# Attention weights of the second head mixing moved from GpSimd to VectorE, and a quarter of six tiles' score copies moved from VectorE to ScalarE

## The chip, the cores and the metric

One core of one Trainium2 chip. The metric is the device time of one execution in microseconds (us), lower is better. The engines are called as in the profile: PE (TensorE, with PEld for its weight loads), DVE (VectorE), ACT (ScalarE), POOL (GpSimd) and SP (SyncE, which here only issues transfers).

## The reference

Talking-heads attention over B = 2 batches, H = 12 heads, S = 448 positions, D = 64, and two feed-forward blocks behind it:

```python
scores = scale * np.matmul(q, k.transpose(0, 1, 3, 2))
scores = np.einsum('bhij,hg->bgij', scores, w_pre)        # first mixing of heads
scores = scores - np.max(scores, axis=-1, keepdims=True)
attn = np.exp(scores)
attn = attn / (np.sum(attn, axis=-1, keepdims=True) + 1e-09)
attn = np.einsum('bhij,hg->bgij', attn, w_post)           # second mixing of heads
out = np.matmul(attn, v)
# then x @ w_gate, silu, * (x @ w_val), @ w_out; then @ w_in, hard-swish, @ w_out
```

## The kernel before

**Two phases.** The attention runs over the first 206 us or so of the execution, the two feed-forward blocks (products of float32 split into a high and a low part) over the rest. Only the attention is touched by the change.

**Tiles and chunks.** The 448 query rows of each batch are cut into four tiles of 88 to 120 rows (`TILES`, t = 0 to 7 over both batches). `scores(t, c)` computes the scores of a pair of heads c (0 to 5) of tile t on PE into two PSUM banks, one for the even head (e = 0) and one for the odd (e = 1). `scores_out(t, c)` copies both banks into the tile's buffer `S0` or `S1` in SBUF (even tiles use `S0`, odd ones `S1`): the bank of e = 0 on DVE, that of e = 1 on ACT. The two banks carry the tag `pqk` with two buffers in all, so the next scores, or the next `av` (the product with v, same tag), wait for both copies.

**Relayout.** The mixing of heads wants heads on partitions. A chunk m is ten query rows; 90 chunks in all. `relayout(m)` moves eight of them from S to a buffer `sx` with a DMA issued on SP, `relayout_rest(m)` the last two with a DMA issued on POOL. Both need the whole tile copied out, the buffer of five pairs earlier free, and an earlier transfer landed that used the same semaphore. The rest of a tile is issued one step later than the tile's first part in program order (`i > scored[...]`).

**The step loop.** Step i (45 of them, two chunks each) issues in this order: `postmix(i)` (second mixing: 64 small matmuls on PE, 32 for each chunk, of the exponentials `e` with the chunk's weights `wn`); `exps` of the two chunks of step i + 1 (ACT); `attn_out(i)` (one copy on DVE, one on ACT); `weights` of the first chunk of step i + 1; the scores that are due in this step, with their copies; `weights` of the second chunk; `premix(i + 2)` (first mixing, PE, from `sx`) and two `row_max` (DVE); `av` where due; and at the step's end the copies `x_out` (DVE), the splits `x_split` (POOL, L324 and L326) and the relayouts. Each engine takes its instructions in that order. `weights(m)` is a chain: L242 adds 1e-9 to the sum, L243 takes the reciprocal (both DVE), and L245 multiplies the 128 x 60 table `W2` by it to give `wn`, on POOL. So POOL's queue holds L245, the splits and the DMA issues of `relayout_rest` in one line.

Scores of tiles 2 to 7 are spread over steps 2-7, 8-13, 13-17, 19-24, 24-29 and 30-35, `av` over 21 of the 45 steps, two pairs of heads each.

Of the kernel before, what the change touches and what calls it, by code (L numbers as in the profile page):

```python
# [12 lines left out]
ALU = mybir.AluOpType  # L13
# [34 lines left out]
def kernel(  # L48
# [14 lines left out]
    nc = tc.nc  # L63
# [66 lines left out]
    W2 = cst.tile([128, H, KG], F32, name="W2")  # L130
# [46 lines left out]
    def scores_out(t, c):  # L177
        n = TILES[t // 4][t % 4][2] * KI
        for e in range(2):
            h = 2 * c + e  # L180
            copy = nc.scalar.copy if e else nc.vector.tensor_copy
            copy(stiles[t][:n, h, :], pqk.pop((t, h))[:n, :S])  # L182

    sx = {}
# [54 lines left out]
    def weights(m):  # L239
        sm = ew[m][1]  # L240
        rc = pe.tile([128, 1], F32, name=f"rc{m}", tag="rc", bufs=6)
        nc.vector.tensor_scalar(rc, sm, 1e-9, None, ALU.add)  # L242
        nc.vector.reciprocal(rc, rc)  # L243
        wn = pe.tile([128, H, KG], F32, name=f"wn{m}", tag="wn", bufs=6)
        nc.gpsimd.tensor_scalar(wn, W2, rc, 1.0, ALU.mult, ALU.mult)  # L245
        wns[m] = wn

    def postmix(i):
# [227 lines left out]
    for t in range(2):  # L476
        for c in range(HP):
            scores(t, c, ("pqk", "ppre", "ppost", "ppre")[(6 * t + c) % 4])
            scores_out(t, c)
        if t == 0:  # L480
            load_q(0, 2, 3)
            for _ in range(8):
                relayout(placed)
                relayout_rest(placed)
                placed += 1
# [14 lines left out]
    def qk(t, c):  # L500
        scores(t, c)
        scores_out(t, c)
# [50 lines left out]
    for i in range(-LOOK, NP):  # L553
# [7 lines left out]
        for m in soft[:1]:  # L561
            weights(m)
        run(i, "qk")
        for m in soft[1:]:
            weights(m)
# [178 lines left out]
```

## Time and profile before

| What | us |
|---|---|
| median of three runs | 717.46 |
| lowest, highest | 711.99, 725.3 |
| the profiled execution's own time | 713.29 |
| its span, first to last instruction | 711.5 |
| PE busy in the span | 685.4 (96%) |
| DVE busy | 503.4 (71%) |
| ACT busy | 296.9 (42%) |
| POOL busy | 176.5 (25%) |

The profile is of one execution. Busy shares are means over two phases with different limits. A "wait" is idle time in front of an instruction, put down to what ended last before it. In the timelines the first column is the start in us from the span's start, the second how long the instruction, or the merged run of alike instructions (x8), took, and the bracket is the idle time before it with its releaser. PE's ends are modelled and overlap the next start, so PE's rows are read from start to start.

### The profile page before, as it was taken

The page shows a single profiled execution, that of the slowest core. Times are in us where ns is not written, and L with a number is a line of the kernel's source. Part 1 is how long each engine was busy: PE and PEld are TensorE (multiplying, and loading weights), DVE is VectorE, ACT ScalarE, POOL GpSimd, SP SyncE. Part 2 cuts the span into 40 slices and gives each one's busy share as a digit, 9 for nine tenths or more (in the row PEclk, how much of TensorE's full clock was granted, in tenths as well). Part 3 has the DMA queues.
Part 4 walks back from the last instruction along what each step waited for, and adds up shares of the span by engine and source line. Part 5 has one row for each costly group of instructions (what it writes and reads, how often), then busy time and mean ns, then how long its engine had stood idle before and what let it go on. Part 6 is the DMA issues. An engine that isn't in the chain of part 4 may idle for free.

```text
span 711.5 us, 16611 instructions
## 1 busy us (share of the span) xinstructions
PE 685.4 (96%) x6864; PEld 571.6 (80%) x6864; DVE 503.4 (71%) x853; ACT 296.9 (42%) x563; POOL 176.5 (25%) x275
## 2 busy tenths in 40 slices
PE   9699899799899999999999999999999999999997
PEld 3355565465579999999999999999999999999997
DVE  4676677688745888888888665668888888765550
ACT  4565466456543433434343322334445544333320
POOL 2444265454640221131112000002332332000000
PEclk9999999899999999999999999999999999999999
DMA  5777456443421424323242334232323323544420
GB/s 198 225 204 202 134 138 180 136 145 84 132 92 46 134 89 133 121 101 130 93 131 92 119 106 132 89 92 92 127 89 96 127 82 100 162 145 145 136 72 27
DMA packets 33629, 86.75 MB, mean 122 GB/s; under 512 B 9264, under 2 KB 21952, under 8 KB 33552
## 3 DMA queue, kind: packets, MB, share of 16 engines
q1 hardware_dynamic: 25632, 80.97, 35.3%
q0 software_dynamic: 7200, 3.94, 2.8%
q8 instruction: 54, 0.88, 0.5%
q10 hardware_dynamic: 720, 0.77, 0.3%
q14 instruction: 23, 0.19, 0.1%
HBM read 62.20 MB, written 2.75 MB: 91 GB/s over the span
## 4 chain that ended last, share of the span: by engine, by line
PE 87%; DMA 5%; issue 2%; DVE 2%; ACT 2%; POOL 1%; SPq 0%; POOLq 0%; ACTq 0%
PE pi L394 16%; PE pp L394 16%; PE po L394 12%; PE pg L394 12%; PE pv L394 12%; PE ppost L259 5%; PE pav L295 5%; PE pqk L166 4%; PE ppre L217 3%; DMA sx<-S 3%; DMA k<-in_k_dram 1%; PE p L394 1%; ACT e L236 1%; DMA q<-in_q_dram 1%; POOL wn L245 1%
## 5 line engine op out<-in xcount | busy, mean ns | idle before, releaser
L394 PE MATMUL pp<-g,hp 128*128 128x448 f32 x384 | 109.1, 365 | 0.0
L605 POOL TENSOR_TENSOR g<-rl,g 128x448 fp32r<-128x448 f32 x32 | 41.5, 1318 | 168.5 <-ACT g L604 168.5
L394 PE MATMUL po<-u,ho 128*128 128x448 f32 x288 | 81.7, 364 | 0.0
L236 ACT ACTIVATE e<-ppre,nm 128x448 f32<-128x448 f32 x90 | 56.4, 631 | 52.8 <-DVE nm L230 52.7
L259 PEld LDWEIGHTS ppost<-wn,e 60*64 60x64 f32 x2880 | 49.5, 137 | 34.3 <-POOL wn L245 29.7
L394 PEld LDWEIGHTS pp<-g,hp 128*128 128x128 f32 x384 | 72.0, 187 | 5.8
L605 POOL TENSOR_TENSOR u<-sg,u 128x448 fp32r<-128x448 f32 x24 | 32.9, 1391 | 151.2 <-ACT u L604 151.2
L394 PE MATMUL pi<-x2h,li 128*128 128x448 f32 x192 | 70.2, 366 | 0.0
L394 PE MATMUL pi<-x2l,hi 128*128 128x448 f32 x192 | 70.0, 364 | 0.0
L394 PE MATMUL pi<-x2h,hi 128*128 128x448 f32 x192 | 69.9, 364 | 0.0
L394 PE MATMUL pp<-g,lp 128*128 128x448 f32 x192 | 69.3, 361 | 0.0
L259 PE MATMUL ppost<-wn,e 60*64 60x60 f32 x2880 | 56.1, 224 | 12.5 <-POOL wn L245 11.3
L206 POOL DMA_DIRECT2D sx<-S x90 | 54.5, 606 | 33.9 <-issue 11.0
L230 DVE TENSOR_REDUCE nm<-ppre 128x1 f32<-128x448 f32 x90 | 51.7, 613 | 12.7 <-PE ppre L217 12.0
L394 PEld LDWEIGHTS po<-u,ho 128*128 128x128 f32 x288 | 54.1, 188 | 3.8
L217 PE MATMUL ppre<-sx,W 64*64 64x448 f32 x360 | 51.1, 558 | 4.6 <-DMA sx<-S 4.6
L166 PE MATMUL pqk<-k,q 64*64 64x448 f32 (+4 forms) x384 | 51.5, 570 | 2.6 <-ACT S L182 2.0
L394 PE MATMUL po<-u,lo 128*128 128x448 f32 x144 | 52.3, 363 | 0.0
L394 PE MATMUL pg<-xl,hg 128*128 128x448 f32 x138 | 50.5, 366 | 0.0
L394 PE MATMUL pv<-xl,hv 128*128 128x448 f32 x138 | 50.5, 366 | 0.0
L394 PE MATMUL pg<-xh,hg 128*128 128x448 f32 x138 | 50.5, 366 | 0.0
L295 PEld LDWEIGHTS pav<-at,v 128*64 128x64 f32 x768 | 36.9, 137 | 16.9 <-ACT S L182 11.8
(105 smaller groups left out, 1369.3 us busy)
## 6 DMA issues: line engine op xcount, KB each, us to landing
sx<-S SPq DMA_DIRECT2D x90, 182.0 KB
ri<-in_moe_w_in_dram SPq DMA_DIRECT2D x16, 768.0 KB
rg<-in_moe_w_gate_dram SPq DMA_DIRECT2D x12, 768.0 KB
rv<-in_moe_w_val_dram SPq DMA_DIRECT2D x12, 768.0 KB
ro<-in_moe_w_out_dram SPq DMA_DIRECT2D x12, 768.0 KB
rp<-in_moe_w_out_dram SPq DMA_DIRECT2D x12, 640.0 KB
rp<-in_moe_w_out_dram SPq DMA_DIRECT2D x6, 768.0 KB
sx<-S POOLq DMA_DIRECT2D x90, 42.0 KB, 4.9
```

The lines of the kernel that those rows point to most:

```text
L166: nc.tensor.matmul(p[e][lo:hi, :S], lhsT=qs[b][r, base + lo : base + hi], rhs=ks[b][r, c, :], start=True, stop=True, tile_position=(64 * e ...
L206: nc.gpsimd.dma_start(out=sx[m // 2][104:128, m % 2, :], in_=rows[8:, :H, :])
L217: nc.tensor.matmul(p[a][64 * r : 64 * r + 64, :S], lhsT=W1[rows, :], rhs=x[rows, r, :], start=True, stop=True, tile_position=(64 * a, 64 * r),
L230: nc.vector.tensor_reduce(nm, pre[m][:, :S], AX.X, ALU.max, negate=True)
L236: nc.scalar.activation(e[:, :S], pre.pop(m)[:, :S], AF.Exp, bias=tot.pop(m), scale=1.0, accum_out=sm)
L245: nc.gpsimd.tensor_scalar(wn, W2, rc, 1.0, ALU.mult, ALU.mult)
L259: nc.tensor.matmul(p[s][64 * c : 64 * c + 64, r, b, :, :], lhsT=e[rows, k0 : k0 + 64], rhs=wn[rows, :, :], start=True, stop=True, tile_pos ...
L295: nc.tensor.matmul(p[64 * e : 64 * e + 64, :n], lhsT=vs[b][:, jc, h, :], rhs=ats[t][:, jc, h, :n], start=jc == 0, stop=jc == JC - 1, tile_ ...
L394: nc.tensor.matmul(p[:, :S], lhsT=wt[:, kk, :], rhs=xx, start=start, stop=stop)
L605: eng.tensor_tensor(to[1], src, to[0].bitcast(F32), ALU.subtract)
```

## The change

Two edits. `weights` issues L245 on DVE, right behind the reciprocal, instead of on POOL. `scores_out` gives both copies to ACT for every odd pair of heads (c = 1, 3, 5) of tiles 2 to 7; that is 18 copies of e = 0 taken from DVE. Nothing else differs.

```diff
@@ scores_out
-            copy = nc.scalar.copy if e else nc.vector.tensor_copy
+            copy = nc.scalar.copy if e or (t > 1 and c % 2) else nc.vector.tensor_copy
             copy(stiles[t][:n, h, :], pqk.pop((t, h))[:n, :S])
@@ weights
         nc.vector.tensor_scalar(rc, sm, 1e-9, None, ALU.add)
         nc.vector.reciprocal(rc, rc)
         wn = pe.tile([128, H, KG], F32, name=f"wn{m}", tag="wn", bufs=6)
-        nc.gpsimd.tensor_scalar(wn, W2, rc, 1.0, ALU.mult, ALU.mult)
+        nc.vector.tensor_scalar(wn, W2, rc, None, ALU.mult)
         wns[m] = wn
```

On DVE, in step 15 (scores of tile 4, pair of heads 3; `rc32` and `wn32` belong to chunk 32):

```order
 L242 TENSOR_SCALAR rc32_1568<-sm32_1562 128x1
 L243 RECIPROCAL rc32_1568<-rc32_1568 128x1
-L182 COPY S0_107<-pqk4_3_0_1573 110x448
+L245 TENSOR_SCALAR wn32_1571<-W2_102,rc32_1568 128x60
 L242 TENSOR_SCALAR rc33_1581<-sm33_1564 128x1
 L243 RECIPROCAL rc33_1581<-rc33_1581 128x1
+L245 TENSOR_SCALAR wn33_1584<-W2_102,rc33_1581 128x60
 L230 TENSOR_REDUCE nm34_1592<-ppre17_0_1586 128x1
 L230 TENSOR_REDUCE nm35_1594<-ppre17_1_1587 128x1
```

The score copy has left DVE's line, and each reciprocal is followed by its own multiplication. In a step with an even pair the copy stays between the two groups and only the multiplications are added.

On POOL, from step 23 to step 26, where tile 5 (buffer `S1`) begins to be relaid (`sx28` holds chunks 56 and 57, its first two; `xh` and `xl` are the splits):

```order
-L245 TENSOR_SCALAR wn48_2241<-W2_102,rc48_2238 128x60
-L245 TENSOR_SCALAR wn49_2254<-W2_102,rc49_2251 128x60
 L324 TENSOR_TENSOR xl0_1520<-xs1_1334,xh0_1519 128x3x120
-L245 TENSOR_SCALAR wn50_2331<-W2_102,rc50_2328 128x60
-L245 TENSOR_SCALAR wn51_2352<-W2_102,rc51_2349 128x60
 L326 CAST xh0_1519<-xs2_1850 128x3x120
-L245 TENSOR_SCALAR wn52_2419<-W2_102,rc52_2416 128x60
-L245 TENSOR_SCALAR wn53_2432<-W2_102,rc53_2429 128x60
 L324 TENSOR_TENSOR xl0_1520<-xs2_1850,xh0_1519 128x3x120
 L206 DMA sx28_2367<-S1_108 24x1x448 x2
 L206 DMA sx29_2370<-S1_108 24x1x448 x2
```

What is left on POOL are splits and relayouts alone; the multiplications that stood in front of them, each behind a reciprocal of DVE, are gone.

## Rows read from the trace of the kernel before

**Rows 1.** The page, part 2: granted PE clock in 40 slices of 17.8 us.
```profile
PEclk9999999899999999999999999999999999999999
```

**Rows 2.** Stretch: busy us of PE, PEld, DVE, ACT, POOL; clock, DMA share, GB/s.
```profile
20.00:206.00 186.00, 165.60 (x4160) 101.36 (x4160) 132.90 (x398) 107.98 (x269) 95.05 (x198) 0.97 0.54 157
206.00:711.50 505.50, 501.11 (x2570) 463.48 (x2568) 362.08 (x441) 181.27 (x282) 75.12 (x57) 1.00 0.33 106
```

**Rows 3.** Timeline of step 15 into step 16: DVE, POOL and PE.
```profile
88.85 0.67 DVE L283 COPY at<-ppost 128x480 f32<-128x480 f32 x1 [0.81 <-PE ppost L259]
...
89.69 0.61 DVE L182 COPY S<-pqk 110x448 f32<-110x448 f32 x1
89.98 0.31 POOL L245 TENSOR_SCALAR wn<-W,rc 128x60 f32<-128x60 f32 x1 [0.30 <-DVE rc L243]
...
90.34 1.46 PE L259 MATMUL ppost<-wn,e 60*64 60x60 f32 x64
...
90.75 0.31 POOL L245 TENSOR_SCALAR wn<-W,rc 128x60 f32<-128x60 f32 x1 [0.46 <-DVE rc L243]
...
91.85 0.67 DVE L283 COPY at<-ppost 128x480 f32<-128x480 f32 x1 [0.25 <-PE ppost L259]
```

**Rows 4.** Timeline of PE: first mixings (ppre) of steps 26, 27, 32 and 33.
```profile
133.03 0.91 PE L217 MATMUL ppre<-sx,W 64*64 64x448 f32 x2
136.97 2.64 PE L217 MATMUL ppre<-sx,W 64*64 64x448 f32 x6 [3.03 <-DMA sx<-S]
...
142.35 1.29 PE L217 MATMUL ppre<-sx,W 64*64 64x448 f32 x8
...
161.51 1.47 PE L217 MATMUL ppre<-sx,W 64*64 64x448 f32 x6
163.93 0.96 PE L217 MATMUL ppre<-sx,W 64*64 64x448 f32 x2 [0.95 <-DMA sx<-S]
...
166.92 0.93 PE L217 MATMUL ppre<-sx,W 64*64 64x448 f32 x8
```

**Rows 5.** Timeline, 123 to 134 us: ACT's copy of tile 5's last pair, then POOL.
```profile
123.57 0.53 ACT L182 COPY S<-pqk 120x448 f32<-120x448 f32 x1
...
130.11 0.31 POOL L245 TENSOR_SCALAR wn<-W,rc 128x60 f32<-128x60 f32 x1 [0.47 <-DVE rc L243]
...
131.28 2.38 POOL L206 DMA_DIRECT2D sx<-S  x4
```

**Rows 6.** DMA issues, 0 to 210 us: KB each, median us from issue to landing.
```profile
sx<-S POOLq DMA_DIRECT2D x90, 42.0 KB, 4.9
```

**Rows 7.** Timelines of PE and POOL: waits at steps 3 and 38.
```profile
33.49 1.06 PE L259 MATMUL ppost<-wn,e 60*64 60x60 f32 x32 [2.79 <-POOL wn L245]
...
183.54 0.60 POOL L245 TENSOR_SCALAR wn<-W,rc 128x60 f32<-128x60 f32 x2
183.92 1.16 PE L259 MATMUL ppost<-wn,e 60*64 60x60 f32 x64 [1.53 <-POOL wn L245]
...
187.05 0.96 PE L217 MATMUL ppre<-sx,W 64*64 64x448 f32 x2 [0.62 <-DMA sx<-S]
```

**Rows 8.** Groups by line, 0 to 206 us: busy us, mean ns | idle before.
```profile
L182 DVE COPY S<-pqk 120x448 f32<-120x448 f32 (+3 forms) x48 | 29.5, 615 | 20.0 <-PE pqk L166 12.9 <-DMA sx<-S 4.0 <-PE ppre L217 1.9
...
L245 POOL TENSOR_SCALAR wn<-W,rc 128x60 f32<-128x60 f32 x90 | 27.7, 312 | 63.1 <-DVE rc L243 46.6 <-DVE rc L242 8.8 <-PE ppre L217 4.8
L182 ACT COPY S<-pqk 120x448 f32<-120x448 f32 (+3 forms) x48 | 25.6, 534 | 17.3 <-PE pqk L166 11.6 <-DMA sx<-S 4.2
...
L242 DVE TENSOR_SCALAR rc<-sm 128x1 f32<-128x1 f32 x90 | 12.7, 141 | 0.5 <-ACT e L236 0.5
```

**Rows 9.** DVE beside POOL in the second phase: timeline at 261 us.
```profile
261.16 0.55 DVE L368 TENSOR_SCALAR yg<-yg 128x768 f32<-128x768 f32 x1
261.39 2.79 POOL L605 TENSOR_TENSOR u<-sg,u 128x448 fp32r<-128x448 f32 x2 [10.91 <-ACT u L604]
261.75 1.41 DVE L369 TENSOR_SCALAR yg<-yg 128x768 uint32<-128x768 uint32 x1
```

## The prediction

> **What bounds the kernel now.** I read the busy times by stretch first. The last 505.5 us are TensorE alone: it is busy for 501.1 of them [rows 2], and no instruction of that phase changes. What the attention gains or loses should therefore reach the end one to one. In the 186 us from 20 to 206 no engine is full: PE 165.6, DVE 132.9, ACT 108.0, POOL 95.1 [rows 2]. So I went on to the timelines, and there two kinds of step differ.
>
> An ordinary step without a product with v is set by a round trip. In step 15 DVE copies `at` at 88.85, runs the first reciprocal, the score copy (89.69 to 90.30) and the second reciprocal; POOL multiplies the second weights at 90.75; the second mixing, a run of 1.16 where nothing holds it up [rows 7], is stretched to 1.46 by them; and the next `at` copy starts at 91.85, 3.00 later, after DVE had idled 0.25 for PE [rows 3]. PE's own work there is a run of 1.16 [rows 7], one of 0.93 for the first mixing [rows 4] and an equal one for the scores, 3.02 in all; the ends are modelled and each overlaps the next run's start by near 0.2, so 2.5 is my estimate.
>
> A few steps are far longer. The first mixing of step 26 starts at 133.03, and after two matmuls stops until 136.97 for a transfer into `sx`; the next step's starts at 142.35, 9.32 later instead of about 3 [rows 4]. Part of that is the clock: the slice from 124.5 to 142.3 is granted 8 tenths where its neighbours have 9 or more [rows 1], and the six matmuls after the wait take 2.64 where eight take 0.93 a little later [rows 4]. The transfer is late because of POOL. Tile 5 is copied out by 124.2 (the last copy starts at 123.57), but POOL issues its first two-row transfers only at 131.28, behind two multiplications that wait for DVE (the second at 130.11) and a split [rows 5]. The landing takes 4.9 [rows 6], and 131.28 plus 0.6 of issue plus 4.9 is 136.8, just when PE goes on.
>
> **The change part by part.**
>
> *The multiplication on DVE.* No row shows it there. From below: DVE's one-element operation takes 0.141 [rows 8] and its 768-element one 0.55 [rows 9], so 60 elements come to 0.141 + 59 x 0.41/767 = 0.173. From above: POOL's 0.312 [rows 8]. I take 0.18 and 0.02 of gap, 0.20, nearer the DVE rows. 90 of them are 18 us of DVE. Against it stands the hand-over: the reciprocal ends at about 89.77 and POOL's result at 90.29 [rows 3], so each weight comes about 0.3 earlier than now when DVE is next in line for it.
>
> *Score copies to ACT.* 18 copies of 0.615 leave DVE, 11.1 us; ACT gets 18 of 0.534, 9.6 us [rows 8]. DVE's balance is +6.9. ACT has about 78 us idle in the stretch [rows 2], which covers 9.6, except where the next scores wait for these very banks: twice (steps 13 and 24) an odd pair is followed by another pair in the same step. I charge 0.5 for the two together (from 0 to 2 x 0.53). Tile 5, for one, is complete 0.53 later for the same reason.
>
> *Ordinary steps.* By the loops of the code 24 of 45 steps have no product with v. In ten of them (3, 5, 7, 9, 15, 20, 22, 29, 31, 35) the pair of heads is odd: DVE's line is 2.75 busy now, less 0.53 (the copy, overlaps counted) plus 0.40 is 2.62, against PE's 2.50; the step falls from 3.00 to about 2.7, gain 10 x 0.3 = 3.0. In twelve others (0, 1, 2, 4, 10, 16, 26, 32, 37, 38, 41, 43) DVE only gets the 0.40: 2.75 + 0.40 = 3.15, loss about 0.2 each, 2.4. The 21 steps with a product with v have 32 more matmuls on PE, which hide it. Net gain 0.6; with each of these sizes off by half it lies between -3 and +4.
>
> *POOL set free.* This is where I see the gain. Without the multiplications POOL's queue no longer keeps pace with DVE: it issues a tile's rows as soon as the tile is copied out and the buffer is free.
> - Steps 26 to 27: issue moves from 131.28 to about 125, landing to about 131, before PE asks at 133. The excess is 9.32 - 3.0 = 6.3, the slow clock in it; I count 5.5, since PE may come for it up to 0.8 earlier. (Bounds: 0 if another transfer is last too, 6.3.)
> - Steps 32 to 33, tile 6: 161.51 to 166.92 is 5.41 [rows 4], excess 2.4; the same reason; I count 2.0 (0 to 2.4).
> - Step 38: the second mixing waits 1.53 for weights that stand behind POOL's transfers [rows 7]; I count 1.2. In the same step the first mixing waits 0.62 for `sx` [rows 7]; in step 32 a wait of 0.95 went with an excess of 2.4 [rows 4], so by that ratio 1.5; I count 1.3. (Together 0 to 3.0.)
> - Step 3: 2.79 lost, because the copies of tile 2 into `S0` wait until tile 0's last rows have left it [rows 7]. POOL can issue those about 2 us earlier, but SP moves the other eight rows of each chunk and I cannot see those land; I count 1.5 (0 to 3.5, with the clock behind it).
>
> Sum: 5.5 + 2.0 + 1.2 + 1.3 + 1.5 = 11.5 from POOL, 0.6 from the steps, less 0.5: 11.6. The profiled execution took 713.3, so 701.7. The median of the three runs, 717.46, stands 4.2 above that execution. Late landings are a likely part of what differs between runs, and the change takes away much of their effect, so I do not carry the 4.2 over and forecast 702.
>
> *A rule against it.* In the second phase DVE's L369 takes 1.41 while POOL's L605 runs, and the like operation just before it 0.55 [rows 9]. The Trainium skill, SBUF — State Buffer, section Who interferes with whom, says that VectorE in its two-port modes, which `tensor_scalar` from SBUF to SBUF can enter, and GpSimd share one port pair and that the later one blocks fully; by that rule, the trace agrees. The new multiplication is such an operation and could wait for a split or a transfer's issue on POOL. By that rule a few of the 90 would each lose some tenths; what that costs at most is worked out in the second rival.
>
> **The rivals.**
>
> *The waits for `sx` stay.* POOL's rows come earlier, but SP's eight rows of a chunk, or the DMA engines themselves (busy share 0.54 in the stretch [rows 2]), are as late. For it: SP waits for the same complete tile, which now comes 0.53 later. Against: issue time and landing of POOL's own rows explain 136.8 by themselves. Then only step 38's 1.2 and the steps' 0.6 less 0.5 are left: 713.3 - 1.3 = 712.
>
> *DVE becomes the bound.* If the score copies were never on the path and DVE's line were it in all steps, the balance of +6.9 would be paid: 720. If besides each multiplication that meets a long POOL operation waited like L369 (0.86 more than its neighbour [rows 9]), say one in ten of the 90, 9 x 0.86 = 7.7 more: 728. It decides from the point where DVE has no idle time in front of the `at` copy; now it has 0.25 in such a step [rows 3], and 53 us over the stretch [rows 2], which speaks against it. Place: the steps with even pairs and those after the scores are done.
>
> *More than counted.* Every excess vanishes (6.3 + 2.4 + 3.0 + 3.5 = 15.2) and the steps give 4: 713.3 - 19 = 694. For it: each of these waits has POOL's queue in front of it; against: shorter steps ask for the transfers sooner.
>
> **How the numbers follow.** Forecast (696 to 708) 0.65, waits stay 0.20, DVE the bound 0.08, more than counted 0.07. A difference of 2% is about what a measurement of this kernel can tell from no change. Measured from the median that line is at 703, from the profiled execution at 699, so it runs through the forecast: I give 0.35 of its 0.65 to faster and 0.30 to same. Faster 0.35 + 0.07 = 0.42; the first rival is all same, and of the second 0.03: same 0.30 + 0.20 + 0.03 = 0.53; slower 0.05. The range of 694 to 713 leaves out the second rival and the ends.
>
> **What would show it.** Right: POOL's transfers for tile 5 start within 2 us after ACT's last copy of that tile; PE's waits for `sx` (3.03, 0.95, 0.62) and the clock's dip at 124.5 to 142.3 are gone; the multiplication on DVE takes 0.17 to 0.20; odd steps come every 2.7, even ones every 3.2; the second phase still lasts 505. Wrong: first mixings still wait for transfers issued on SP; the multiplication takes over 0.3; DVE shows no idle time before the `at` copy even in steps with a product with v; or the copies of an odd pair on ACT hold back PE in more than the two steps named.

## The result, and the profile after

The changed kernel takes 710.3 us (median of 20 runs, 704.29 to 714.06); beside it the kernel before took 716.09 (20 runs, 711.99 to 725.3). The ratio is 0.9907, with a 95% interval of 0.9884 to 0.993: 6.7 us faster (0.0093 x 716.1). I had forecast 702. The profiled execution took 714.06, 3.8 above its median, which matters below.

The stretches that answer to [rows 2], and the clock row of the page that answers to [rows 1]:

```profile
20.00:206.00 186.00, 159.52 (x4137) 99.03 (x4138) 146.63 (x469) 114.20 (x286) 67.46 (x108) 0.98 0.53 158
206.00:711.50 505.50, 501.87 (x2602) 464.17 (x2598) 362.12 (x441) 181.18 (x282) 74.15 (x56) 1.00 0.33 106
...
PEclk9999999999999999999999999999999999999999
```

DVE's busy time rose by 13.7 us, ACT's by 6.2, POOL's fell by 27.6. The second phase lasts as before. The clock's dip in the slice from 124.5 us is gone.

What POOL was to give back, it gave. First POOL and ACT at the end of tile 5, then PE's first mixings of steps 26 and 27 (timelines of the kernel after; they answer to [rows 5] and [rows 4]):

```profile
128.82 0.97 ACT L182 COPY S<-pqk 120x448 f32<-120x448 f32 x2
...
130.19 1.24 POOL L206 DMA_DIRECT2D sx<-S  x2 [12.67 <-ACT S L182]
...
138.10 0.93 PE L217 MATMUL ppre<-sx,W 64*64 64x448 f32 x8
...
141.41 0.93 PE L217 MATMUL ppre<-sx,W 64*64 64x448 f32 x8
```

POOL has been idle for 12.67 us and issues 0.40 after ACT's last copy of the tile ended, where it was 7.2 late before. The two first mixings are 3.31 apart instead of 9.32, both in one piece.

But PE now waits for other things. PE's waits from 20 to 206 us, columns: line and releaser, us in total, times, longest; first of before, then of after:

```profile
PE ppost L259 <- POOL wn L245: 11.3, 13, 2.8
PE ppre L217 <- DMA sx<-S: 4.6, 3, 3.0
...
PE pav L295 <- ACT S L182: 0.8, 4, 0.2
PE pqk L166 <- issue: 0.4, 1, 0.4
```

```profile
PE pav L295 <- ACT S L182: 6.4, 9, 1.2
PE ppost L259 <- DVE rc L242: 5.5, 7, 1.2
PE ppost L259 <- issue: 4.7, 3, 2.1
PE ppost L259 <- DVE wn L245: 4.1, 3, 2.5
...
PE pqk L166 <- issue: 1.1, 1, 1.1
```

No wait for `sx` is left. The second mixing's waits for its weights, 11.3 us on POOL before, now end on DVE and are hardly shorter (5.5 + 4.1). Two waits are new: the product with v (`pav`) waits 6.4 us for ACT's score copies, where it was 0.8; and 5.8 us are put down to "issue", a stop that no semaphore explains, where it was 0.4.

An odd step without a product with v came out as worked out. Step 15 of after, DVE, to be held against [rows 3]:

```profile
92.22 0.68 DVE L283 COPY at<-ppost 128x480 f32<-128x480 f32 x1 [0.81 <-PE ppost L259]
...
93.18 0.25 DVE L245 TENSOR_SCALAR wn<-W,rc 128x60 f32<-128x60 f32 x1
...
93.73 0.25 DVE L245 TENSOR_SCALAR wn<-W,rc 128x60 f32<-128x60 f32 x1
...
94.96 0.66 DVE L283 COPY at<-ppost 128x480 f32<-128x480 f32 x1
```

It lasts 2.74 (94.96 - 92.22) instead of 3.00; I had said 2.7. DVE has no idle time in it any more: it sets this step. The even step 16 lasts 3.26, where I had said 3.2.

The groups by line over the whole span, to be held against [rows 8] (busy us, mean ns):

```profile
L182 ACT COPY S<-pqk 120x448 f32<-120x448 f32 (+3 forms) x66 | 33.4, 536 | 16.6 <-PE pqk L166 12.6 <-DMA sx<-S 1.8 <-PE ppre L217 1.4
...
L245 DVE TENSOR_SCALAR wn<-W,rc 128x60 f32<-128x60 f32 x90 | 27.6, 307 | 3.1
L182 DVE COPY S<-pqk 120x448 f32<-120x448 f32 (+3 forms) x30 | 18.6, 622 | 16.7 <-PE pqk L166 11.0 <-DMA sx<-S 4.1 <-PE ppre L217 0.3
```

A multiplication of the weights costs DVE 0.307 in the mean (the median is 0.253; seven of the 90 take 0.50 to 1.80), not 0.18 and a gap of 0.02.

**Where the time went, step by step.** DVE's 45 copies to `at` mark the steps. The table gives, for each class of step, how much the distances between these copies changed against the profile of before, in us; minus is a gain. Step 44 has no following copy and is left out. The first column is my sum sorted in the same way (step 3's 1.5 stands with the third class, since the wait lies between the copies of steps 2 and 3; the 0.2 a step of even steps is shared out).

```
steps                                       predicted  after     e1     e3     e6     e7
26, 32, 37, 38 (waits behind POOL)             -9.2    -8.45  -8.32  -8.68  -8.57  -7.68
3 5 7 9 15 20 22 29 31 35 (odd, no av)         -3.0    -1.70  +3.57  +1.37  -1.45  +2.69
0 1 2 4 10 16 41 43 (other, no av)             +0.1    +3.41  -0.48  -1.13  -0.13  +0.34
13, 24 (two pairs of scores)                   +0.5    -0.52  -0.55  -0.48  -0.02  -0.52
20 steps with a product with v                  0      +8.02  +1.25  -1.86  +0.83  +2.71
sum                                           -11.6    +0.76  -4.53 -10.78  -9.34  -2.46
```

In the profile of after the first class gave nearly what I had counted, and the last took it back. Each column is one execution with stops of its own, so its sum is not the difference of the medians: of the +3.41 of after, 1.78 is step 10, with a stop and a slow clock (last section), and 1.43 is step 43, with a multiplication held up beside POOL (e4). The columns e1, e3, e6 and e7 are experiments.

### The profile page after: what moved, and what is told of

Its sections match the earlier page's. It is cut to its first block, busy times and chain, and to the rows that moved or that the text cites. A ratio compares the mean times of both kernels' runs of the same rounds, so it can differ in the third digit from the quotient of the medians.

```text
span 712.3 us, 16449 instructions
## 1 busy us (share of the span) xinstructions
PE 679.8 (95%) x6864; PEld 570.3 (80%) x6864; DVE 517.3 (73%) x925; ACT 303.1 (43%) x581; POOL 147.9 (21%) x185
## 4 chain that ended last, share of the span: by engine, by line
PE 83%; DVE 8%; DMA 4%; ACT 2%; issue 2%; SPq 0%; POOL 0%; ACTq 0%; DVEq 0%; POOLq 0%
PE pi L394 16%; PE pp L394 16%; PE po L394 12%; PE pg L394 12%; PE pv L394 12%; PE pav L295 4%; PE pqk L166 4%; PE ppost L259 3%; DMA sx<-S 2%; DVE nm L230 2%; PE ppre L217 2%; DVE wn L245 2%; DMA q<-in_q_dram 2%; DVE at L283 1%; ACT e L236 1%
## 5 line engine op out<-in xcount | busy, mean ns | idle before, releaser
L206 POOL DMA_DIRECT2D sx<-S x90 | 52.1, 579 | 110.5 <-ACT S L182 37.2
L166 PE MATMUL pqk<-k,q 64*64 64x448 f32 (+4 forms) x384 | 53.3, 567 | 3.4 <-ACT S L182 1.9
L394 PE MATMUL pv<-xh,hv 128*128 128x448 f32 x138 | 50.4, 365 | 0.0
```

The lines of the kernel that those rows point to most:

```text
L166: nc.tensor.matmul(p[e][lo:hi, :S], lhsT=qs[b][r, base + lo : base + hi], rhs=ks[b][r, c, :], start=True, stop=True, tile_position=(64 * e ...
L206: nc.gpsimd.dma_start(out=sx[m // 2][104:128, m % 2, :], in_=rows[8:, :H, :])
L394: nc.tensor.matmul(p[:, :S], lhsT=wt[:, kk, :], rhs=xx, start=start, stop=stop)
```

## The experiments

Each ratio is against the kernel before on the same chip, with its 95% interval. The full change stands at 0.9907.

### One edit at a time: e1 and e2

```diff
 e1, against before
-        nc.gpsimd.tensor_scalar(wn, W2, rc, 1.0, ALU.mult, ALU.mult)
+        nc.vector.tensor_scalar(wn, W2, rc, None, ALU.mult)
 e2, against before
-            copy = nc.scalar.copy if e else nc.vector.tensor_copy
+            copy = nc.scalar.copy if e or (t > 1 and c % 2) else nc.vector.tensor_copy
```

> Only the weights' multiplication on DVE, score copies as before. Theory 1 (the gain comes from POOL's freed queue, and the ordinary steps get no shorter): PE's wait for sx at step 26, 3.03 before, is below 0.5, the step from first mixing to first mixing there 3.0 to 3.6, and the time is 0.985 to 1.00 of before: like the full change or a little slower, since DVE carries 18 copies more. Rival A (the copies on ACT are what made it faster): 1.00 or above, no better than before. Rival B (DVE's line is the bound): 1.01 or more.

> Only the 18 score copies on ACT, multiplication on POOL as before. Theory 1: PE still waits 2 to 4 us for sx at step 26 and 0.5 to 1.5 at steps 32 and 38; time 0.995 to 1.008 of before. Rival A: 0.985 to 0.995, as the full change.

Measured: e1 0.9971 (0.9949 to 0.9992), 2.1 us; e2 1.0009 (0.9988 to 1.003), nothing. PE's waits in e1, then in e2:

```profile
PE ppost L259 <- DVE wn L245: 5.8, 10, 2.6
PE pav L295 <- ACT S L182: 5.6, 8, 0.7
```

```profile
PE ppre L217 <- DMA sx<-S: 3.7, 4, 1.6
```

The weights on DVE alone take away every wait for `sx`, and the waits for DVE and for `pav` eat most of it. The copies alone leave PE waiting for `sx` (3.7 us, 4.6 before); that what the odd steps gain is waited for there fits this, but no run shows it. Together the edits gain 6.7, more than the 2.1 - 0.6 of the two apart: the copies pay clearly only beside the weights on DVE, which also make the transfers early.

### The transfers early, nothing moved: e3

```diff
-        while rests < placed and rests // 2 <= i + LOOK + 3 and i > scored[chunks[rests][0]]:
+        while rests < placed and rests // 2 <= i + LOOK + 3 and i >= scored[chunks[rests][0]]:
```

POOL issues a tile's two-row transfers one step earlier in its program; the multiplication stays on POOL.

> The kernel before with one comparison changed: the two-row transfers of a new tile are issued on POOL at the end of the step in which the tile is complete, not one step later, so two multiplications fewer stand in front of them; nothing moves between engines. Theory 1: the wait for sx at step 26 falls from 3.03 to under 1, those at steps 32 and 38 to under 0.5, and the time to 0.985 to 0.993 of before, as much as the full change gives, with no load on DVE. Rival A and a rival by which another transfer is last as well: 0.997 to 1.003, the waits stay.

Measured: 0.9875 (0.9841 to 0.9909), 8.9 us, by its middle more than the full change, within overlapping intervals. PE's waits from 20 to 206 us:

```profile
PE pav L295 <- ACT S L182: 1.2, 6, 0.2
...
PE ppre L217 <- DMA sx<-S: 0.5, 2, 0.3
```

The waits for `sx` are nearly gone and nothing took their place. So the early transfers alone give the whole gain, and POOL didn't have to lose the multiplication for it: it only had to take the transfers in another order.

### The full change without its lock: e4

DVE, not POOL, makes the low part of the first two blocks of weights (the subtraction of L385).

```diff
-        eng = nc.gpsimd if pool is pools["wp0"] else nc.vector
+        eng = nc.vector
```

> The changed kernel with the low part of the first two weight blocks subtracted on DVE instead of POOL (steps 42 and 43), so that no POOL operation of 1.8 us stands beside the last multiplications on DVE. Theory (the multiplication of 1.80 and PE's wait of 1.31 at step 44 are the shared port): no multiplication on DVE above 1.1, the wait of 1.31 gone, 0 to 2 us faster than the changed kernel, 0.987 to 0.992 of before. Rival (DVE's own later queue caused the wait): the wait stays within 0.3 of 1.31 and the time is as the changed kernel's or slower by about 1 us, the cost of two subtractions of 0.96 on DVE.

Behind it stood this place of the kernel after, at the end of the attention:

```profile
203.93 1.80 POOL L385 TENSOR_TENSOR lv<-yv,hv 128x768 fp32r<-128x768 f32 x1 [3.17 <-ACT hv L383]
203.98 1.80 DVE L245 TENSOR_SCALAR wn<-W,rc 128x60 f32<-128x60 f32 x1
...
205.84 0.69 PE L259 MATMUL ppost<-wn,e 60*64 60x60 f32 x32 [1.31 <-DVE wn L245]
```

A multiplication of 0.25 takes 1.80 beside a subtraction of POOL that began 0.05 earlier, and PE waits 1.31 for it. Measured in e4: 0.9898 (0.9863 to 0.9932); the multiplication there takes 0.25, and that wait of 1.31 is gone, so the lock is shown; another, of 1.35 at 102 us, stayed, where I had expected none above 1.1. The step from copy 43 to copy 44 is still 1.04 longer than before (1.43 in after), but in e4 most of it ran at the lower clock, granted 0.50 (columns as in [rows 2]):

```profile
197.20:200.40 3.20, 3.20 (x33) 2.37 (x30) 2.38 (x8) 1.33 (x2) 0.00 (x0) 0.50 0.02 5
```

So the step doesn't price the lock. The time can't be told from that of the full change: the middles differ by 0.6 us.

### Both together, and the copies with early transfers: e5 and e6

e5 is the full change with the edit of e3; e6 is e3 with the copies of e2, the weights on POOL.

> The full change, with the two-row transfers written one step earlier in POOL's program as well (the edit of e3). Theory (what the full change gains is the early transfers and nothing else, and it has them already): the ratio stays at that of the full change, 0.991 (0.988 to 0.994), and the wait of TensorE for ACT's score copies in steps with a product with v stays near 6 us. Rival (early transfers and relieved engines are two separate gains that add): 0.9907 x 0.9875, about 0.978.

> The kernel before with the earlier transfers of e3 and the score copies of odd pairs on ACT; the weights stay on POOL. Theory (with the transfers early the path runs over DVE and ACT in turn; copies alone moved nothing, 1.0009, since every gain ended in the waits for the transfers; now DVE's 11.1 us less and ACT's 9.6 us more about cancel): 0.984 to 0.991, the same as e3 within its interval. Rival 1 (the copies relieve DVE, as the way from e1, 0.9971, to the full change, 0.9907, suggests): 4.6 us better than e3, 0.981. Rival 2 (ACT's queue in steps with a product with v is the new bound): 0.993 or more.

Measured: e5 0.9878 (0.9848 to 0.9908), e6 0.9847 (0.9824 to 0.9869). The two gains don't add: e5 is not near 0.978. Its middle is 2 us below the full change, but the intervals overlap. The copies are worth 2.0 us on top of e3 (0.0028 x 714), again within overlapping intervals, and 4.6 on the way from e1 to the full change (0.0064 x 715), where they are clear. e5 against e6 also prices the weights on DVE as the change has them, with early transfers in both: 2.2 us (0.0031 x 714), within overlapping intervals.

### The price of DVE's time alone: e7

```diff
 e7, against e3
         nc.gpsimd.tensor_scalar(wn, W2, rc, 1.0, ALU.mult, ALU.mult)
+        spare = pe.tile([128, H, KG], F32, name=f"spare{m}", tag="spare", bufs=2)
+        nc.vector.tensor_scalar(spare, W2, rc, None, ALU.mult)
```

> The kernel of e3 plus a second, unused multiplication of the weights on DVE behind each reciprocal (90 of them); POOL still makes the weights that are used. It prices DVE's time alone, with hand-over and transfers as in e3. Theory (each pair of multiplications puts the row maxima of the step off by 0.4 to 0.6 us, and with them the exponentials, ACT's copies and the product with v): 5 to 9 us slower than e3, ratio 0.994 to 1.000, and waits of TensorE for ACT's score copies of 4 us or more. Rival (DVE has room, and what e1 lost against e3 is the lock with POOL or the transfers' order): within 2 us of e3, 0.985 to 0.990.

Measured: 0.9953 (0.9932 to 0.9974), 5.6 us slower than e3 (0.0078 x 714). The spare line of the groups, two `at` copies of step 15, and the new wait:

```profile
L247 DVE TENSOR_SCALAR spare<-W,rc 128x60 f32<-128x60 f32 x90 | 22.8, 253 | 3.1
```

```profile
89.62 0.67 DVE L285 COPY at<-ppost 128x480 f32<-128x480 f32 x1 [0.81 <-PE ppost L261]
...
92.92 0.67 DVE L285 COPY at<-ppost 128x480 f32<-128x480 f32 x1
```

```profile
PE pav L297 <- ACT S L182: 3.6, 8, 0.5
```

The step grew from 3.01 (e3) to 3.30, and `pav`'s wait for ACT from 1.2 (e3) to 3.6, a little less than I had expected. So 22.8 us more on DVE, used by nobody and hardly ever locked (none over 0.31), cost 5.6 us: 0.25 of a microsecond for each. This is the price of DVE's time where the weights are still handed over to POOL and DVE makes all copies of e = 0. The change spares the hand-over and the odd pairs' copies, and by e5 against e6 it pays less, 2.2.

### A shorter chain on DVE: e8, e9, e12

```diff
 in the three of them
-        nc.vector.tensor_scalar(rc, sm, 1e-9, None, ALU.add)
-        nc.vector.reciprocal(rc, rc)
+        nc.vector.reciprocal(rc, sm)
```

e8 is the full change with this, e9 is e6 with this, e12 is e5 with this. The addition of 1e-9 is left out in all three; the sum is at least 1 (the row's maximum gives exp(0)), so that in float32 it changes nothing.

> The full change with the addition of 1e-9 ahead of the reciprocal left out (90 DVE instructions of 0.14 us, a part of the computation that is not made); the rest is as in the full change. Theory (DVE's chain reciprocal, weights, row maxima is on the path in most steps): 90 x 0.14 to 0.17 is 13 to 15 us less on DVE, of which about a third to a half reaches the path: 4 to 7 us better than the full change, 0.981 to 0.985, and the waits for ACT's score copies fall from 6.4 to about 4. Rival (DVE is not on the path; ACT's and TensorE's own lines are): 0.989 to 0.993.

> The kernel of e6 (transfers early, score copies of odd pairs on ACT, weights on POOL) with the addition of 1e-9 left out as in e8. Theory (every microsecond taken from DVE ahead of the weights and the row maxima is worth 0.2 to 0.35 us; 13 to 15 us go): 3 to 5 us better than e6, ratio 0.977 to 0.981. Rival (with the weights on POOL, DVE has so much room that its time no longer counts): 0.983 to 0.987, as e6.

> The same with the weights on DVE, as in the change under study (e8 with the transfers one step earlier). Theory (DVE's 27 us of weights cost 0.2 to 0.3 each, less the hand-over to POOL that they spare): 2 to 5 us slower than e9, 0.982 to 0.987. Rival (with a shorter chain on DVE, sparing the hand-over weighs more than DVE's time): as fast as e9 or faster, 0.980 or less.

Measured: e8 0.9842 (0.9818 to 0.9865), e9 0.984 (0.9806 to 0.9875), e12 0.987 (0.984 to 0.99). With the weights on DVE, taking 12.7 us off its chain brings the full change 4.6 us (0.0065 x 715, clear of its interval), somewhat over the 3.2 that e7's price gives; e8's waits for `pav` fell only from 6.4 to 5.6, less than I had expected:

```profile
PE pav L294 <- ACT S L182: 5.6, 8, 0.7
```

With the weights on POOL the same edit brings nothing to be seen (e9 against e6: 0.5 us): the rival held there. And e12 against e5 shows 0.6 us within its interval, though it should have shown e8's 4.6. The three don't agree better than to some 4 us; that DVE's time is on the path rests on e7, and with the weights on DVE on e8, and e12 speaks for a smaller size. e12 against e9, the weights on DVE against those on POOL, is 2.1 us slower (0.003 x 715, within overlapping intervals), as e5 against e6. The fastest of all are e6, e8 and e9, 0.984 to 0.985, which can't be told apart.

### Step 3: e13

```diff
 e13, against e9: the scores of tile 2 at steps 3 to 8
-((2, 7), (8, 13), (13, 17), (19, 24), (24, 29), (30, 35))
+((3, 8), (8, 13), (13, 17), (19, 24), (24, 29), (30, 35))
```

> The kernel of e9 with the six scores of tile 2 at steps 3 to 8 instead of 2 to 7, which asks for S0 one step later. It looks at the wait of 2.5 to 2.8 us in step 3 that my forecast gave 1.5 us back. Theory (tile 0's last rows leave S0 near 32 us by the order of all transfers of the start, whoever issues them; a step later nobody waits for them): the wait of the second mixing at 33 us falls under 0.7, gain 1 to 2.5 us against e9. Rival (the start is bound by the transfers as a whole, so the wait turns up again a step later, or tile 2 now comes late): within 1 us of e9 or slower.

Measured: 0.9865 (0.9837 to 0.9892), no better than e9 and, by the middle, 1.8 us slower. The stretch from copy 2 to copy 3 is 3.41 us shorter than before (0.07 in e9), so the wait at step 3 went; but step 8, which now has two pairs of scores, grew by 2.56, and step 5 by 1.36. The rival held: the time turns up later.

### Stops of TensorE that nothing explains: e14

```diff
 e14, against after: in the first warm-up
+        for _ in range(20 if n == WARM[0] else 0):
+            nc.tensor.matmul(p[:, :16], lhsT=idle[:, :128], rhs=idle[:, :16], start=True, stop=True)
```

> The full change with 20 small extra matmuls (16 columns, and 20 weight loads with them) among TensorE's first warm-up matmuls, before any data has arrived: 40 more instructions on TensorE, nothing else. It looks at the idle times before TensorE's instructions that no semaphore explains: in the full change 2.12, 1.08, 0.54 and 2.05 us, and the same three or four matmuls resume so in e4 and e5 (the last 18, 2 and 53 matmuls of a second mixing, the last four of a pair of scores). Theory (TensorE's own program is fetched in packets of 16 KB, 256 instructions of 64 bytes, and TensorE stops at a packet's first instruction when the packet is late): the places move back by 20 matmuls with their weight loads, so that such idle times are found before the last 38 and the last 22 matmuls of a second mixing and no longer before the last 18, 2 or 53; each ends 1.3 to 1.7 us after a packet of the instruction queue has landed. Rival (they come from something that these instructions wait for and the profile does not show): the places stay, at the last 18, 2 and 53 matmuls. The time: as the full change, 0.988 to 0.994, unless the places now fall on less or more of the path, 2 us either way.

Measured: 0.9896 (0.9865 to 0.9927), as the full change. PE around two of these stops, first in after, then in e14:

```profile
191.88 1.15 PE L259 MATMUL ppost<-wn,e 60*64 60x60 f32 x60
193.57 0.27 PE L259 MATMUL ppost<-wn,e 60*64 60x60 f32 x2 [0.54 <-issue]
...
198.92 0.44 PE L259 MATMUL ppost<-wn,e 60*64 60x60 f32 x11
201.42 1.03 PE L259 MATMUL ppost<-wn,e 60*64 60x60 f32 x53 [2.05 <-issue]
```

```profile
188.53 0.81 PE L259 MATMUL ppost<-wn,e 60*64 60x60 f32 x40
190.44 0.57 PE L259 MATMUL ppost<-wn,e 60*64 60x60 f32 x24 [1.11 <-issue]
...
194.28 1.45 PE L295 MATMUL pav<-at,v 128*64 128x120 f32 x23
198.48 1.16 PE L295 MATMUL pav<-at,v 128*64 128x120 f32 x9 [2.76 <-issue]
```

The stop after 60 of the 64 matmuls of a second mixing (60 + 4) now comes after 40. The one after 11 now comes with 9 left of the 32 of the product before it: 11 + 9 is 20. Both moved back by exactly the 20 matmuls put in. The places belong to the program's order, not to the data. (I had named the places 18 and 2 as ones that should be empty; e14 has a stop before the last 18 and one before the last 2, but at other steps.)

## Why the prediction was wrong

The direction, the mechanism on POOL and the range of 694 to 713 held; the size did not, 6.7 us instead of 11.6, on a median that stood 2.8 above my base. Of the 8.3 us between 702 and 710.3, that base is 2.8; POOL's terms are 2.6 (11.5 counted, 8.9 in e3); the steps and copies are 2.3 (a gain of 0.6 - 0.5 counted, a loss of 8.9 - 6.7 = 2.2 measured). These are middles, each good to some 2 us; the rest is that the medians differ by 5.8 where the ratio says 6.7. That 710.3 lies beside the first rival's 712 is chance, since the waits for `sx` did not stay.

**Right: POOL's queue.** Transfers that start when the tile is complete, waits for `sx` and the dip of the clock gone, 8.45 of 9.2 us in the four steps. e3 shows that this alone gives the whole gain. Of the terms, step 26 gave 4.18 between its `at` copies (I counted 5.5, less 0.2), step 32 gave 2.15 (2.0), steps 37 and 38 gave 2.12 (2.5). **Step 3's 1.5 did not come**: PE still waits there, 2.48 where it was 2.79 [rows 7], because the copies into `S0` still wait for a transfer, and the stretch gained 0.53. Which transfer is last there was not tried. e13 shows that moving this wait away is no gain either.

```profile
31.93 0.62 DVE L182 COPY S<-pqk 120x448 f32<-120x448 f32 x1 [2.30 <-DMA sx<-S]
...
33.15 1.12 PE L259 MATMUL ppost<-wn,e 60*64 60x60 f32 x32 [2.48 <-DVE wn L245]
```

**Wrong: "The 21 steps with a product with v have 32 more matmuls on PE, which hide it."** This is the step that failed: it put the loss in these steps at nothing, and in after they lost 8.02 us. Of that 3.67 are stops and 1.24 a stretch at the lower clock (both below), and 1.11 is step 8, where the score copies waited for a transfer out of `S1`:

```profile
54.78 0.62 DVE L182 COPY S<-pqk 90x448 f32<-90x448 f32 x1 [1.77 <-DMA sx<-S]
```

The 2.0 that are left (about as much in e4's profile: 6.56 less 4.48 of stops) I put down to DVE and ACT. Step 30 of after shows the path:

```profile
152.12 1.15 DVE L230 TENSOR_REDUCE nm<-ppre 128x1 f32<-128x448 f32 x2
...
152.84 0.63 ACT L236 ACTIVATE e<-ppre,nm 128x448 f32<-128x448 f32 x1 [0.55 <-DVE nm L230]
...
153.46 0.62 ACT L236 ACTIVATE e<-ppre,nm 128x448 f32<-128x448 f32 x1
...
154.07 0.64 ACT L283 COPY at<-ppost 128x480 f32<-128x480 f32 x1
...
154.55 0.54 ACT L182 COPY S<-pqk 100x448 f32<-100x448 f32 x1
...
155.15 1.73 PE L295 MATMUL pav<-at,v 128*64 128x110 f32 x32 [0.67 <-ACT S L182]
```

The row maxima begin behind the weights on DVE; ACT's two exponentials wait for them; the copies of `at` and of the scores stand behind these in ACT's queue; and `pav` needs the bank that the score copy frees. PE has more matmuls in such a step, but it can't begin them. What the odd step ahead gained (2.74 for 2.98) was given back here (4.83 for 4.51). That DVE's time does this by itself is shown by e7, where these steps take 4.6 us more than in e3, 0.9 of them a stop; that it goes by way of ACT is read from the timelines and was not tried by itself, and e8, faster with hardly less of this wait, shows that the wait's sum is not its price.

**Mis-sized: the multiplication.** 0.20 with its gap, against 0.307 in the mean: 0.253 undisturbed, the rest beside POOL. The upper bound, POOL's 0.312, would have been the better choice, and at e7's price the 0.107 x 90 = 9.6 us are worth about 2.4, an estimate and rather an upper one. The odd steps, where I counted -3.0, gave -1.7. The rule of the Trainium skill on the shared port pair (SBUF — State Buffer, Who interferes with whom) did apply: 1.80 instead of 0.25 in the worst case, 27.6 - 90 x 0.253 = 4.8 us of DVE in all. Each of the seven long ones ends 0.05 to 0.06 us after an operation of POOL did. What they cost on the path is within the noise of e4 for the longest, and was not tried for the others.

**Right in part: the copies.** The 0.5 of steps 13 and 24 was not lost, and the relief of DVE in the odd steps is seen: -1.70 in after against +3.57 in e1, which lacks it. But e6 against e3, both with the weights on POOL, shows what the forecast left out: in their profiles the odd steps are 2.8 us shorter and the steps with a product with v 2.7 longer. `pav`'s wait for ACT rose there from 1.2 to 2.8:

```profile
PE pav L295 <- ACT S L182: 2.8, 7, 0.7
```

**Wrong: the base.** I did not carry over the 4.2 between the profiled execution and the median, as I took late landings for its cause. The waits for `sx` went and a spread of the same kind stayed (704.29 to 714.06), so they were not its main cause; over the kernels it goes with TensorE's stops (last section), which is no proof. The rival "DVE becomes the bound" was nearer than its 0.08: DVE does bind in the odd steps, yet 0.25 of each microsecond is paid in e7, not all.

By the ratios the parts meet in two ways. -8.9 (e3) + 5.6 (e7) - 2.0 to 4.6 (the copies) is -5.3 to -7.9, and 6.7 was measured. Or -8.9 - 2.0 (e6) + 2.2 (e5 against e6) is -8.7, which is e5, and the full change, whose transfers come one step later in POOL's program, is 2.0 short of it, within overlapping intervals. So DVE's price stays open between 2.2 and 5.6 us.

## What to carry to other kernels

When a transfer is late because its issue stands behind slow work in an engine's queue, try first to issue it earlier in that queue: here one character (e3) gave as much as moving 90 instructions to another engine, without the new owner's bill. An engine with idle time isn't free: follow what stands behind the added instruction through the next engines' queues up to the bottleneck, and price it with a spare copy of the instruction (e7) as well as with the swap itself (e5 against e6): here they gave 5.6 and 2.2 us. And where one profiled execution stands off the median, look for what differs before choosing the base.

## What the runs showed of the hardware

**TensorE stops for its own program.** The instruction queue moves packets of 16,384 bytes, 54 of them in each execution:

```profile
q8 instruction: 54, 0.88, 0.5%
```

54 x 16,384 bytes over 13,728 matmuls and weight loads (6864 of each on the page) are 64.4 bytes for one, so a packet holds some 256 instructions. In the profiles of the 14 kernels, before and after among them, TensorE stopped 40 times between 15 and 215 us for 0.3 us or more (up to 2.76) with "issue" as the releaser, and each time it went on 1.19 to 1.76 us after such a packet had landed, though only 33 or 34 of them come in these 200 us, one every 6 us. Counted over all of TensorE's instructions in the trace (matmuls, weight loads and the waits of its sequencer), all 40 stops stand at the same place of 256: 193 or 194 instructions behind a multiple of 256, in every one of the 14 kernels. The kernels after, e4 and e5, whose TensorE programs are alike, stop at the same matmuls (e5 at all four places of after, e4 at three), and e14 moves the matmuls there but not the count. So these stops are waits for the program itself. Most of the places are passed without one; why a packet comes late was not tried. The kernel before has 0.4 us of them, after 5.8. Over the 14 kernels the profiled execution's time less the median goes with their sum: -2.8 to -4.7 in before, e1, e2 and e12 (0.4 to 1.4 us of stops), +1.6 to +6.4 in after, e4, e5, e9, e13 and e14 (4.5 to 6.5 us); the correlation is 0.81. This goes together over the runs and is no experiment.

**The clock fell behind some of these stops.** In after the stop of 2.12 us that ended at 67.14 was followed by a stretch at the lower of the two clock levels, 1.2 instead of 2.4 GHz, granted 0.50 from 67.2 us for 3.4 us (the columns as in [rows 2]):

```profile
62.00:68.00 6.00, 3.88 (x82) 2.04 (x80) 3.24 (x11) 3.26 (x10) 1.14 (x2) 0.93 0.77 204
68.00:74.00 6.00, 6.00 (x84) 2.53 (x81) 3.28 (x11) 2.94 (x7) 1.15 (x2) 0.78 0.79 205
```

With it steps 10 and 11 lost 3.03 us, and the profiled execution is the slowest of the 20 runs of after. The clock fell likewise, to 0.50, behind a stop of 1.82 us in e3, one of 2.33 in e4, and ones of 1.77 and 2.05 in e5; in e14 it fell towards the end of one of 2.76. It stayed at 1.00 behind a stop of 2.05 in after (at 201.42) and one of 1.87 in e14, so such a stop alone does not decide it; what else does was not tried.
